# Feed-forward slots issued in pairs: two up products, then two down products, in one fixed order on TensorE

## The chip, the cores and the metric

The kernel runs on one core of one Trainium2 chip. The metric is the device time of one execution in microseconds (us), lower is better. Five engines work side by side, each through its own instructions in a fixed order: PE (TensorE, matrix products), ACT (ScalarE), DVE (VectorE), POOL (GpSimd) and SP (SyncE, which only issues transfers). They wait for one another by semaphores.

## The reference

Attention over 8 batches, 8 heads, 576 positions and 64 features, with a mask that is local (32 back) for the first four heads and strided (every 32nd position) for the others; its output becomes 4608 tokens of 512 features, which go through a feed-forward layer with a squared ReLU.

```python
scores = scale * np.matmul(q, k.transpose(0, 1, 3, 2))
mask_local = (rel >= 0) & (rel < stride)
mask_strided = (rel >= 0) & (pos[None, :] % stride == pos[:, None] % stride)
...
x = attn_out.transpose(0, 2, 1, 3).reshape(B * S, H * D)   # 4608 x 512
h = np.maximum(x @ w_in, 0.0)                              # w_in 512 x 2048
return h * h @ w_out                                       # w_out 2048 x 512
```

## The kernel before

The 4608 tokens are cut into 12 chunks of 384, and the 2048 hidden features into 16 tiles of 128. One chunk with one tile is a slot; slot s = 16 c + j belongs to chunk c and tile j, and there are 192 of them. float32 values are split into a high and a low part (x into xlh, xll, xsh, xsl: l for the local heads, s for the strided ones, the last letter for the part; weights and hidden values in the same way), and each product is made of three matmuls: high by high, high by low, low by high.

- `up(c, j)`, called U(s) in this text, makes the hidden tile h of a slot: 12 matmuls of 384 columns on PE (line 430) into one PSUM bank, then on ACT a relu (435), a square (436) and a copy to gh (437), then on DVE gl = h - gh (438). The bank is `j % 2` in chunk 0, so two banks in turn, and one of three in later chunks. gh and gl come from `gpool`, which holds two of each.
- `down(c, j)`, D(s), multiplies gh and gl with w_out: 9 matmuls of 512 columns (line 450) into three PSUM banks y that gather the 16 slots of the chunk. After the last slot of a chunk, DVE and ACT copy y out (454) and SP issues the three output transfers.
- The attention of chunk c+1 is made while chunk c goes through the feed-forward layer. The local heads (`pe_head`: matmuls s on line 231 and o on line 273, and around them ACT, DVE and POOL) and the strided ones (`strided`: products on POOL, pq and pp, sums on DVE) are generators; after each slot the loop advances them by a share.
- In chunk 0 the loop also converts the weights (`convert`): on ACT a first step z (162), a scaling of raw words (150) and a copy w (169), two steps on DVE (165, 166) and one on POOL (170), two cuts of 512 columns per slot.

What the program writes is then put in order by a list scheduler: on each engine it takes what is ready in its own estimate, and among that what was written first. So the loop's order gives priorities, not a fixed sequence. Down products lag by two slots:

```python
for s in range(NS + 2):
    c, j = divmod(s, NFT)
    if s < NS:
        up(c, j)
    if s >= 2:
        down(*divmod(s - 2, NFT))
    # then: weights in chunk 0, and a share of the attention of chunk c + 1
```

Of the kernel before, what the change touches and what calls it, by code (L numbers as in the profile page):

```python
# [23 lines left out]
TC = 384  # L24
WP = 512
NCHUNK = NT // TC
NFT = DF // P
# [20 lines left out]
def f32(ap):  # L48
    return ap.bitcast(F32)
# [23 lines left out]
def ranges(c):  # L73

    res = []
    for s, (b, g) in enumerate(SEGS[c]):
        if res and res[-1][0] == b and res[-1][2] == SI * g:
            res[-1][2] += SI
        else:
            res.append([b, SI * g, SI * (g + 1), SEG * s])  # L80
    return res
# [3 lines left out]
def attn_moe(ctx: ExitStack, tc, qk_l, v_l, qk_d, v_d, qk_p, v_p, f_s, q_s, k_s, v_s, w_in, w_out, masks, eye, out):  # L85
    nc = tc.nc
# [13 lines left out]
    def psum(i, nm):  # L100

        return ps.tile([P, 512], F32, name=nm, tag=f"ps{i}")
# [16 lines left out]
    last = {}  # L119
# [298 lines left out]
    g_tiles, y_ps = {}, {}  # L418

    def up(c, j):  # L420
        x = xt[c]
        p, o = divmod(j, 2)
        ph = psum(j % 2 if c == 0 else (c * NFT + j) % 3, f"h{c}_{j}")
        n = 0
        for kt in range(4):
            kind, kk = "ls"[kt // 2], kt % 2
            xh, xl = x[kind, "h"][:, kk, :], x[kind, "l"][:, kk, :]
            wsl = slice(kt * 256 + o * P, kt * 256 + (o + 1) * P)
            for w, xx in ((wi[p][0], xh), (wi[p][0], xl), (wi[p][1], xh)):
                nc.tensor.matmul(ph[:, :TC], w[:, wsl], xx, start=n == 0, stop=n == 11)  # L430
                n += 1
        gh = gpool.tile([P, TC], F32R, name=f"gh{c}_{j}", tag="gh")
        gl = gpool.tile([P, TC], F32R, name=f"gl{c}_{j}", tag="gl")
        g = ph[:, :TC]
        nc.scalar.activation(g, g, AF.Relu)  # L435
        nc.scalar.activation(g, g, AF.Square)  # L436
        nc.scalar.copy(gh, g)  # L437
        nc.vector.tensor_sub(gl, g, f32(gh))  # L438
        g_tiles[c, j] = gh, gl

    def down(c, j):
        gh, gl = g_tiles.pop((c, j))
        p, o = divmod(j, 2)
        if j == 0:
            y_ps[c] = [ps_y.tile([P, DM], F32, name=f"y{c}_{t}", tag="psy") for t in range(NTT)]
        wsl = slice(o * DM, (o + 1) * DM)
        for t in range(NTT):
            sl = slice(t * P, (t + 1) * P)
            for k, (g, w) in enumerate(((gh, wo[p][0]), (gh, wo[p][1]), (gl, wo[p][0]))):
                nc.tensor.matmul(y_ps[c][t], g[:, sl], w[:, wsl], start=j == 0 and k == 0, stop=j == NFT - 1 and k == 2)  # L450
        if j == NFT - 1:
            for t in range(NTT):
                y = ypool.tile([P, DM], F32, name=f"ysb{c}_{t}", tag="ysb")
                (nc.scalar.copy if t == 1 else nc.vector.tensor_copy)(y, y_ps[c][t])
                nc.sync.dma_start(out=out[c * TC + t * P : c * TC + (t + 1) * P, :], in_=y)


    def run(gen):
        for _ in gen:
            pass  # L460

    def behind(ins, gen):

        while True:
            with ExitStack() as st:
                for i in ins.values():
                    st.enter_context(tc.issue_after(i.ins))
                try:
                    k = next(gen)
                except StopIteration:  # L470
                    return
            yield k
# [25 lines left out]
    def local(c):  # L498
        if c < NPLAIN:
            heads = [pair_at(c, pr, True, pr, "34") for pr in range(2)]  # L500
            turns = (0, 0, 1, 0, 1, 0, 0, 1, 1, 1)
        else:
            heads = [pe_head(c, h) for h in range(HL)]

            turns = [0] * 3
            for h in range(HL):
                turns += [h] + [h + 1] * (3 if h + 1 < HL else 0) + [h] * 2
        for h in turns:
            next(heads[h])
            yield  # L510
# [53 lines left out]
    NS = NCHUNK * NFT  # L564
    for s in range(NS + 2):
        c, j = divmod(s, NFT)
        if s < NS:
            up(c, j)
        if s >= 2:
            down(*divmod(s - 2, NFT))  # L570
        if c == 0:
            for _ in range(WRATE):
                if next(weights, "end") != "end":
                    weights_end = {e: last[e] for e in "agsv"}
        if c + 1 < NCHUNK:
            if j == 0:
                lo, st = local(c + 1), strided(c + 1)
                if c == 0:
                    lo, st = behind(heads_end, lo), behind(heads_end, st)
                if c == 1:  # L580
                    lo, st = behind(weights_end, lo), behind(weights_end, st)
                cost = sum(2 * sum(range(i0 + 1, i1 + 1)) + 10 for _, i0, i1, _ in ranges(c + 1))
                dl = ds = 0
            fl, fs = ((j + 1) / n for n in SPREAD[min(c, 1)])
            while dl < fl * (10 if c + 1 < NPLAIN else 6 * HL) and next(lo, "end") != "end":
                dl += 1
            while ds < fs * cost:
                k = next(st, "end")
                if k == "end":
                    break  # L590
                ds += k
            if j == NFT - 1:
                run(lo)
                run(st)
# [76 lines left out]
```

## Time and profile before

| | |
|---|---|
| median of 3 runs | 903.3 us (903.24 to 903.33) |
| the profiled execution, its own time | 902.66 us |
| its span | 900.8 us |
| PE busy | 886.3 us (98%) |
| POOL busy | 693.4 us (77%) |
| DVE busy | 669.5 us (74%) |
| ACT busy | 564.4 us (63%) |
| granted PE clock, mean | 0.982 of full speed |

The span runs from the first to the last instruction; the profiled execution took 1.9 us more than its span. In rows of single groups a time stands before the engine; "x2" means two instructions of that kind in a row, and what stands in square brackets is the idle time before them and what ended it.

### The profile page before, as it was taken

The page shows a single profiled execution, that of the slowest core. Times are in us where ns is not written, and L with a number is a line of the kernel's source. Part 1 is how long each engine was busy: PE and PEld are TensorE (multiplying, and loading weights), DVE is VectorE, ACT ScalarE, POOL GpSimd, SP SyncE. Part 2 cuts the span into 40 slices and gives each one's busy share as a digit, 9 for nine tenths or more (in the row PEclk, how much of TensorE's full clock was granted, in tenths as well). Part 3 has the DMA queues.
Part 4 walks back from the last instruction along what each step waited for, and adds up shares of the span by engine and source line. Part 5 has one row for each costly group of instructions (what it writes and reads, how often), then busy time and mean ns, then how long its engine had stood idle before and what let it go on. Part 6 is the DMA issues. An engine that isn't in the chain of part 4 may idle for free.

```text
span 900.8 us, 14866 instructions
## 1 busy us (share of the span) xinstructions
PE 886.3 (98%) x4744; PEld 800.0 (89%) x4744; DVE 669.5 (74%) x1840; ACT 564.4 (63%) x1458; POOL 693.4 (77%) x724
## 2 busy tenths in 40 slices
PE   8989999999999999999999999999999999999997
PEld 7778899999999999999989989999999999999996
DVE  6789668878877878878878887887886887885111
ACT  3898967657657657747746755755665765764332
POOL 5788577788788889989879997988899799785000
PEclk8599999999999999999999999999999999999999
DMA  9833441323113114102212311221131111000000
GB/s 352 346 123 126 129 150 35 121 69 104 51 51 112 47 48 139 43 13 98 75 32 69 104 31 54 59 86 60 28 110 47 46 46 68 25 1 2 35 1 35
DMA packets 26798, 71.41 MB, mean 79 GB/s; under 512 B 2976, under 2 KB 8736, under 8 KB 25184
## 3 DMA queue, kind: packets, MB, share of 16 engines
q1 hardware_dynamic: 26432, 70.14, 23.4%
q8 instruction: 37, 0.61, 0.3%
q10 hardware_dynamic: 288, 0.33, 0.1%
q14 instruction: 41, 0.34, 0.1%
HBM read 61.01 MB, written 9.44 MB: 78 GB/s over the span
## 4 chain that ended last, share of the span: by engine, by line
PE 86%; POOL 5%; DVE 5%; ACT 2%; issue 1%; DVEq 0%; POOLq 0%; ACTq 0%
PE h L430 41%; PE y L450 40%; POOL pp L402 2%; PE s L231 2%; PE o L273 2%; POOL pq L380 1%; DVE sc L381 1%; DVE px L263 1%; PE b L308 1%; DVE p_t L256 1%; PE w_ps L525 1%; PE b L335 0%; POOL kx L215 0%; DVE e L312 0%; DVE nm L313 0%
## 5 line engine op out<-in xcount | busy, mean ns | idle before, releaser
L450 PE MATMUL y<-w,gh 128*128 128x512 f32 x1152 | 361.9, 395 | 2.4 <-ACT gh L437 2.4
L450 PEld LDWEIGHTS y<-w,gh 128*128 128x128 f32 x1152 | 212.6, 189 | 35.0 <-ACT gh L437 2.6
L430 PE MATMUL h<-xlh,w 128*128 128x384 f32 x768 | 232.7, 342 | 0.4 <-DVE xsl L351 0.4
L430 PE MATMUL h<-xsh,w 128*128 128x384 f32 x768 | 228.1, 337 | 0.0
L402 POOL TENSOR_TENSOR pp<-vs,sc 128x448 f32<-128x448 f32 (+10 forms) x192 | 193.6, 1034 | 39.9 <-issue 21.7
L450 PE MATMUL y<-w,gl 128*128 128x512 f32 x576 | 223.7, 395 | 0.0
L380 POOL TENSOR_TENSOR pq<-ks,qs 128x512 f32<-128x512 f32 (+2 forms) x192 | 200.1, 1063 | 16.0 <-DVE sc L381 12.4
L381 DVE TENSOR_REDUCE sc<-pq 128x8 f32<-128x512 f32 (+4 forms) x228 | 120.1, 535 | 61.4 <-POOL pq L380 59.7
L435 ACT ACTIVATE h<-h 128x384 f32<-128x384 f32 x192 | 91.0, 475 | 112.6 <-PE h L430 111.5
L438 DVE TENSOR_TENSOR gl<-h,gh 128x384 fp32r<-128x384 f32 x192 | 105.4, 549 | 61.4 <-ACT gh L437 59.9
L430 PEld LDWEIGHTS h<-xlh,w 128*128 128x128 f32 x768 | 142.9, 189 | 8.4 <-DVE xsl L351 0.7
L430 PEld LDWEIGHTS h<-xsh,w 128*128 128x128 f32 x768 | 142.5, 189 | 0.5 <-ACT w L169 0.3
L403 DVE TENSOR_REDUCE qs<-pp 128x64 f32<-128x448 f32 (+11 forms) x192 | 106.8, 563 | 31.7 <-POOL pp L402 29.6
L430 PE MATMUL h<-xll,w 128*128 128x384 f32 x384 | 130.3, 339 | 0.0
L430 PE MATMUL h<-xsl,w 128*128 128x384 f32 x384 | 129.2, 336 | 0.0
L450 PEld LDWEIGHTS y<-w,gl 128*128 128x128 f32 x576 | 108.0, 188 | 20.8
L437 ACT CAST gh<-h 128x384 fp32r<-128x384 f32 x192 | 91.2, 475 | 34.1 <-PE y L450 30.3
L436 ACT ACTIVATE h<-h 128x384 f32<-128x384 f32 x192 | 91.0, 474 | 4.5
L240 ACT ACTIVATE e<-e,nm 96x128 f32<-96x128 f32 x160 | 62.6, 392 | 28.3 <-DVE nm L223 27.0
L430 PEld LDWEIGHTS h<-xll,w 128*128 128x128 f32 x384 | 72.8, 190 | 7.5
L256 DVE STREAM_TRANSPOSE p_t<-e 32x128 f32<-32x128 f32 x240 | 72.2, 301 | 4.8 <-ACT e L245 1.4
L430 PEld LDWEIGHTS h<-xsl,w 128*128 128x128 f32 x384 | 72.7, 189 | 0.2
(82 smaller groups left out, 1113.6 us busy)
## 6 DMA issues: line engine op xcount, KB each, us to landing
qk<-qk_l SPq DMA_DIRECT2D x24, 400.0 KB, 3.1
y<-ysb SPq DMA_DIRECT2D x36, 256.0 KB, 2.3
raw<-w_in SPq DMA_DIRECT2D x7, 1024.0 KB, 11.1
qk<-qk_l SPq DMA_DIRECT2D x16, 416.0 KB, 3.1
vs<-v_s SPq DMA_DIRECT2D x10, 576.0 KB, 3.8
raw<-w_out SPq DMA_DIRECT2D x5, 1024.0 KB, 13.3
v<-v_l SPq DMA_DIRECT2D x40, 128.0 KB, 2.0
ks<-k_s SPq DMA_DIRECT2D x8, 576.0 KB, 3.7
```

Of the source, the lines that this page charges most:

```text
L240: nc.scalar.activation(e[:QC, cut(w)], e[:QC, cut(w)], AF.Exp, bias=nmax[:QC, w : w + 1], scale=-1.0, accum_out=ssum[:QC, w, :1])
L256: nc.vector.transpose(out=pt[STR * k : STR * (k + 1), :, STR * r : STR * (r + 1)], in_=e.rearrange("p (w k) -> p w k", k=KW)[STR * r : STR ...
L380: nc.gpsimd.tensor_mul(pv, kt[:, a : a + m, :], qt[:, i - i0 : i - i0 + 1, :].broadcast_to([P, m, D]))
L381: nc.vector.tensor_reduce(out=sc[:, i - i0, a : a + m], in_=pv, op=ALU.add, axis=AX.X)
L402: nc.gpsimd.tensor_mul(pv, vt[:, a : a + nd, :n], sc[:, il : il + 1, :n].broadcast_to([P, nd, n]))
L403: nc.vector.tensor_reduce(out=ot[:, il, a : a + nd], in_=pv, op=ALU.add, axis=AX.X)
L430: nc.tensor.matmul(ph[:, :TC], w[:, wsl], xx, start=n == 0, stop=n == 11)
L435: nc.scalar.activation(g, g, AF.Relu)
L436: nc.scalar.activation(g, g, AF.Square)
L437: nc.scalar.copy(gh, g)
L438: nc.vector.tensor_sub(gl, g, f32(gh))
L450: nc.tensor.matmul(y_ps[c][t], g[:, sl], w[:, wsl], start=j == 0 and k == 0, stop=j == NFT - 1 and k == 2)
```

## The change

The loop now issues at every even s two up products, U(s) and U(s+1), and then two down products, D(s-2) and D(s-1). Each group of two is written inside `tc.issue_after` of the last matmul of the group before it, which makes the scheduler put all of the group's instructions on PE behind that one. For that, `up` and `down` return their last matmul. Inside a group the scheduler is still free, and so it is with the attention's instructions. The weights and the attention are advanced after each s as before.

```diff
-        if s < NS:
-            up(c, j)
-        if s >= 2:
-            down(*divmod(s - 2, NFT))
+
+        if s % 2 == 0:
+            for part, slots in (up, (s, s + 1)), (down, (s - 2, s - 1)):
+                with ExitStack() as behind_last:
+                    if "ff" in last:
+                        behind_last.enter_context(tc.issue_after(last["ff"].ins))
+                    for i in slots:
+                        if 0 <= i < NS:
+                            last["next"] = part(*divmod(i, NFT))
+                last["ff"] = last["next"]
```

In the rows below a name is a tile with chunk and slot (h0_2 is the hidden tile of chunk 0, slot 2; gh0_0, gl0_0 the split one of slot 0), followed by a running number. Line 450 of before is line 451 now.

On PE, at the first slots, behind U(0), U(1) and four matmuls of attention (b), before:

```order
L308 MATMUL b11_0_1_619<-qk1_0_1_552 96x128 x4
L450 MATMUL y0_0_663<-w1_0_421,gh0_0_532 128x512 x2
L450 MATMUL y0_1_664<-w1_0_421,gh0_0_532 128x512 x2
L450 MATMUL y0_2_665<-w1_0_421,gh0_0_532 128x512 x2
L430 MATMUL h0_2_644<-xlh0_435,w0_1_407 128x384
L430 MATMUL h0_2_644<-xll0_436,w0_1_407 128x384
```

and at the same place now:

```order
L308 MATMUL b11_0_1_619<-qk1_0_1_571 96x128 x4
L430 MATMUL h0_2_644<-xlh0_435,w0_1_407 128x384
L430 MATMUL h0_2_644<-xll0_436,w0_1_407 128x384
L430 MATMUL h0_2_644<-xlh0_435,w0_1_407 128x384 x2
L430 MATMUL h0_2_644<-xll0_436,w0_1_407 128x384
L430 MATMUL h0_2_644<-xlh0_435,w0_1_407 128x384
```

The six matmuls of D(0) with gh have moved from ahead of U(2) to behind U(3); U(2) writes the bank that U(0) used.

On ACT, in chunk 0 from the relu of slot 5 on, before:

```order
L435 ACTIVATE h0_5_830<-h0_5_830 128x384
L162 ACTIVATE z8_512_868<-raw8_680 128x512
L169 CAST w1_3_858<-raw8_680 128x512
L436 ACTIVATE h0_5_830<-h0_5_830 128x384
L437 CAST gh0_5_843<-h0_5_830 128x384
```

and now:

```order
L435 ACTIVATE h0_5_779<-h0_5_779 128x384
L162 ACTIVATE z8_512_868<-raw8_708 128x512
L169 CAST w1_3_858<-raw8_708 128x512
L436 ACTIVATE h0_5_779<-h0_5_779 128x384
L437 CAST gh0_4_773<-h0_4_760 128x384
```

The copy gh of slot 4, which stood ahead of the relu of slot 5, now stands behind relu, z, w and square of slot 5; gh of slot 5 comes four instructions later.

On PE, at the border from chunk 3 to chunk 4 (h4_0 is U(64), y3 with gh3_14 is D(62)), before:

```order
L430 MATMUL h4_0_3920<-xlh4_3248,w0_0_395 128x384
L430 MATMUL h4_0_3920<-xll4_3249,w0_0_395 128x384
L430 MATMUL h4_0_3920<-xlh4_3248,w0_0_395 128x384 x2
L450 MATMUL y3_0_3222<-w1_7_1270,gh3_14_3877 128x512 x2
L450 MATMUL y3_0_3222<-w1_7_1270,gl3_14_3878 128x512
L450 MATMUL y3_1_3223<-w1_7_1270,gh3_14_3877 128x512 x2
L430 MATMUL h4_0_3920<-xll4_3249,w0_0_395 128x384
```

and now:

```order
L430 MATMUL h4_0_3920<-xlh4_3276,w0_0_395 128x384
L231 MATMUL s05_0_4020<-kx5_0_3991,qx5_0_3990 96x256 x2
L231 MATMUL s25_0_4026<-kx5_0_3991,qx5_0_3990 96x256 x2
L430 MATMUL h4_0_3920<-xlh4_3276,w0_0_395 128x384
L430 MATMUL h4_1_3939<-xlh4_3276,w0_0_395 128x384
L430 MATMUL h4_1_3939<-xll4_3277,w0_0_395 128x384
L430 MATMUL h4_1_3939<-xlh4_3276,w0_0_395 128x384 x2
L430 MATMUL h4_0_3920<-xll4_3277,w0_0_395 128x384
```

The five matmuls of D(62) that stood inside U(64) are gone from there; four of U(65) and the s matmuls of the next chunk's first head stand in their place.

More of the change, by code (lines that the diff above doesn't have):

```diff
@@ L429, in up @@
             for w, xx in ((wi[p][0], xh), (wi[p][0], xl), (wi[p][1], xh)):
-                nc.tensor.matmul(ph[:, :TC], w[:, wsl], xx, start=n == 0, stop=n == 11)
+                done = nc.tensor.matmul(ph[:, :TC], w[:, wsl], xx, start=n == 0, stop=n == 11)
                 n += 1
@@ L439, in up @@
         g_tiles[c, j] = gh, gl
+        return done
     def down(c, j):
@@ L449, in down @@
             for k, (g, w) in enumerate(((gh, wo[p][0]), (gh, wo[p][1]), (gl, wo[p][0]))):
-                nc.tensor.matmul(y_ps[c][t], g[:, sl], w[:, wsl], start=j == 0 and k == 0, stop=j == NFT - 1 and k == 2)
+                done = nc.tensor.matmul(y_ps[c][t], g[:, sl], w[:, wsl], start=j == 0 and k == 0, stop=j == NFT - 1 and k == 2)
         if j == NFT - 1:
@@ L455, in down @@
                 nc.sync.dma_start(out=out[c * TC + t * P : c * TC + (t + 1) * P, :], in_=y)
+        return done
     def run(gen):
```

## The prediction

> **What bounds the kernel now.** U(s) and D(s) are the twelve up matmuls and the nine down matmuls of slot s. I read the page first.
>
> ```profile
> span 900.8 us, 14866 instructions
> ...
> PE 886.3 (98%) x4744; PEld 800.0 (89%) x4744; DVE 669.5 (74%) x1840; ACT 564.4 (63%) x1458; POOL 693.4 (77%) x724
> ...
> PE 86%; POOL 5%; DVE 5%; ACT 2%; issue 1%; DVEq 0%; POOLq 0%; ACTq 0%
> ```
>
> PE is busy for 98% of the span, and 86% of the chain of waits is PE. A busy PE can hide pauses, so the windows (after its span each row has busy us and count by engine, then PE's granted clock) and PE's waits came next.
>
> ```profile
> 46.00:61.00 15.00, 12.64 (x64) 11.07 (x64) 13.39 (x31) 12.98 (x25) 11.15 (x13) 0.89 0.31 99
> 61.00:71.00 10.00, 10.00 (x54) 8.36 (x53) 8.62 (x19) 10.00 (x20) 10.00 (x13) 1.00 0.65 222
> 116.00:186.00 70.00, 70.00 (x368) 63.66 (x367) 54.91 (x174) 45.71 (x128) 55.82 (x67) 1.00 0.29 92
> 824.00:901.00 77.00, 71.69 (x357) 64.24 (x355) 11.96 (x21) 24.48 (x52) 1.32 (x1) 0.98 0.06 21
> ```
>
> ```profile
> PE y L450 <- ACT gh L437: 2.4, 1, 2.4
> ...
> PE o L273 <- DVE px L263: 1.3, 1, 1.3
> ```
>
> From 61 us on PE never rests within these windows; behind its start it waits twice worth naming, 2.4 us for gh(0) and 1.3 us for an attention head. Whatever makes PE wait anywhere is therefore paid in full, and at most 3.7 us can be won back. Last, the spacing of matmuls where no attention is left:
>
> ```profile
> 851.52 0.33 PE L430 MATMUL h<-xsh,w 128*128 128x384 f32 x1
> 851.69 0.63 PE L450 MATMUL y<-w,gh 128*128 128x512 f32 x2
> ...
> 853.54 0.39 PE L450 MATMUL y<-w,gl 128*128 128x512 f32 x1
> 853.77 0.33 PE L430 MATMUL h<-xlh,w 128*128 128x384 f32 x1
> ```
>
> U to D takes 0.17 us from start to start and D to U 0.23, which is (853.77-851.69)/9 = 0.23 again: a change from U to D costs nothing. U takes 12 x 0.175 = 2.1 us, D 2.08.
>
> **The change part by part.** No instruction is added or removed. Half the joins between U and D go (192 of them): worth 0 by the rows above. What changes is what stands between a producer and its consumer. gpool holds two gh and two gl, so gh(s) on ACT waits for the end of D(s-2) in either version. In chunk 0 two PSUM banks hold h, so U(s+2) waits for gl(s). Before, U(s+1) and D(s-1) lay in between, 4.2 us; now only D(s-1) does, 2.08 us.
>
> *A, the start.* U(2) now stands ahead of D(0), and needs the bank that gl(0) frees.
>
> ```profile
> 48.69 0.48 ACT L437 CAST gh<-h 128x384 fp32r<-128x384 f32 x1
> ...
> 49.23 2.93 PE L450 MATMUL y<-w,gh 128*128 128x512 f32 x6 [2.35 <-ACT gh L437]
> ...
> 50.88 0.55 DVE L438 TENSOR_TENSOR gl<-h,gh 128x384 fp32r<-128x384 f32 x1
> ...
> 51.96 0.42 PE L430 MATMUL h<-xlh,w 128*128 128x384 f32 x1
> ```
>
> ```profile
> 45.30:48.70 3.40, 1.57 (x11) 1.11 (x10) 1.79 (x4) 3.27 (x9) 1.41 (x2) 1.00 0.22 54
> 48.70:52.10 3.40, 2.87 (x7) 2.30 (x8) 3.40 (x9) 2.57 (x6) 2.31 (x2) 0.50 0.19 73
> 52.10:55.50 3.40, 3.40 (x20) 3.18 (x19) 3.33 (x11) 2.85 (x6) 2.63 (x3) 1.00 0.31 46
> ```
>
> ACT and DVE have the same order up to gl(0), which ends at 50.88+0.55 = 51.43. So U(2) starts near 51.5. At 51.96 the six matmuls of D(0) are missing (6 x 0.23 = 1.4 us at full clock) and 0.46 us of U(2) at half clock (0.2) are there: 1.2 us lost. Then the clock: a stretch of 3.4 us with PE busy for 1.57 was followed by one at 0.50, one with 2.87 by one at 1.00. Now 48.7 to 52.1 holds some 0.6 us, so 52.1 to 55.5 should run at half clock: 3.4/2 = 1.7 us more. Bounds: 1.2 (the clock comes up anyway) and 4.6 (one more such stretch). I take 1.2+1.7 = 2.9, since 0.6 is nearer to 1.57 than to 2.87. The Trainium skill's page "TensorE: Matmul & The Clock Gate", section "What's actually happening", has the clock fall only after an idle window of about 3.4 us. Here it fell behind a window that was 46% busy, so the row decides; by the page A would be 1.2 and the whole sum 1.7 us less.
>
> *B, the other bank waits of chunk 0*, U(4) to U(15), twelve of them. How late gl(s) comes behind the end of D(s-2), at the shortest (s=9) and the longest (s=8) of slots 2 to 15:
>
> ```profile
> 88.57 0.86 PE L450 MATMUL y<-w,gl 128*128 128x512 f32 x3
> 89.78 0.48 ACT L437 CAST gh<-h 128x384 fp32r<-128x384 f32 x1
> 90.30 0.56 DVE L438 TENSOR_TENSOR gl<-h,gh 128x384 fp32r<-128x384 f32 x1
> ...
> 83.16 0.86 PE L450 MATMUL y<-w,gl 128*128 128x512 f32 x3
> 86.60 0.47 ACT L437 CAST gh<-h 128x384 fp32r<-128x384 f32 x1
> 89.10 0.52 DVE L438 TENSOR_TENSOR gl<-h,gh 128x384 fp32r<-128x384 f32 x1
> ```
>
> ```profile
> L169 ACT CAST w<-raw 128x512 fp32r<-128x512 f32 x24 | 15.7, 652 | 0.0
> L162 ACT ACTIVATE z<-raw 128x512 uint32<-128x512 uint32 x23 | 14.6, 636 | 2.4 <-DVE raw L166 2.4
> L435 ACT ACTIVATE h<-h 128x384 f32<-128x384 f32 x16 | 7.8, 486 | 6.0 <-PE h L430 6.0
> ```
>
> That is 90.86-89.43 = 1.4 us and 89.62-84.02 = 5.6 us. Against 2.08 us of cover the shortest costs 0, the longest 3.5: bounds 0 and 12 x 3.5 = 42. Much of the long one goes, because relu and square of slot s now run under U(s+1) and D(s-2) and only gh and gl are left: gh 0.48, gl 0.55, half an instruction in flight on each engine (0.33, 0.28), hand-overs 0.15, together 1.8, just under the cover. But ACT is full here (10.00 of 10.00 us). In the pairs 2, 4, 8 and 12 a relu of slot s+1, a z and a w stand between square(s) and gh(s): from the end of U(s+1), 0.48+0.65+0.64 = 1.8 and in three of them a square of 0.48, so ACT reaches gh(s) about when D(s-2) ends, if it began on time, and any lateness of ACT is PE's. I let one release in each of four pairs wait for one more ACT instruction, 0.7 us: 2.8. It is nearer to the short end.
>
> *C, chunk borders.* Before, D(s-2) could run between the matmuls of U(s) when x of the new chunk was late; now U(s+1) stands ahead of it. POOL's last write of x against PE, chunks 7 to 8 and 3 to 4:
>
> ```profile
> 612.33 1.02 POOL L281 TENSOR_TENSOR xll<-e,xlh 64x384 fp32r<-64x384 f32 x1
> ...
> 613.26 0.63 PE L450 MATMUL y<-w,gh 128*128 128x512 f32 x2
> ...
> 614.88 0.34 PE L430 MATMUL h<-xll,w 128*128 128x384 f32 x1
> ```
>
> ```profile
> 326.52 1.01 POOL L281 TENSOR_TENSOR xll<-e,xlh 64x384 fp32r<-64x384 f32 x1
> ...
> 328.62 0.63 PE L450 MATMUL y<-w,gh 128*128 128x512 f32 x2
> ```
>
> Without the filler PE would need xll at 613.26, 0.1 us before it is there, and at 328.62, 1.1 us after. By the order, the last head's o stands 1.9 and 3.4 us of U and D work later than before there; the new chunk's s matmuls (0.5) and in the second case four of U(s+1) (0.7) fill. That leaves 0.1+1.9-0.5 = 1.5 and 3.4-1.1-0.5-0.7 = 1.1. The tightest of the other borders is the last, where the strided part of x is late:
>
> ```profile
> 823.48 1.85 POOL L414 TENSOR_TENSOR xsl<-ks,xsh 128x768 fp32r<-128x768 f32 x1 [1.88 <-ACT xsh L413]
> ...
> 825.49 0.63 PE L450 MATMUL y<-w,gh 128*128 128x512 f32 x2
> ```
>
> It lands at 825.33, 0.16 us before PE would need it without filler; six of U(177) now fill 1.05, and PE's lag of A and B gives POOL, which has a queue of its own here, more room. Minus the 1.3 us of PE's wait for o, which stands twelve matmuls later: C = 1.3, from -1.3 to 8 (eleven borders of 0.7).
>
> *No price:* in later chunks three banks hold h and the tighter release has 4.2 us of cover; on SP's queue the output transfers keep their places, and loads of q and k pass them by one to three places, mostly forward; nothing of U or D runs on POOL. ACT now often waits for two D in a row with gh(s) and gh(s+1), and attention's exps queue behind; ACT is busy 45.71 of 70.00 there, so I count its price in C alone.
>
> Sum: 2.9+2.8+1.3 = 7.0 us. The profiled execution took 902.66 us, 0.64 under the median of the runs, 903.30: 902.66+0.64+7.0 = 910.3.
>
> **The rivals.**
> - *No change.* The clock is up at 52.1, no release in B is late and C is 0: 903.3+1.2 = 904.5. For it: the 1.8 us under the cover. Against: ACT at 10.00 of 10.00. It is in force when gl(s) comes within 2.08 us each time.
> - *Faster.* A join costs up to 0.01 us, the last digit of the rows: 192 x 0.01 = 1.9, and the wait for o goes, 1.3: 903.3-3.2 = 900.1. It decides once A and B together are under 1.4 us, which needs gl(0) right behind gh(0), near 49.8. DVE has other work there.
> - *ACT's lag carries over.* Every release of B waits as the middle slot of before would (3.8 us late, less 2.08, 1.7): 12 x 1.7 = 20 instead of 2.8, 927. For it: ACT was full. Against: relu and square are out of that chain.
> - *The clock falls in chunk 0.* If waits bunch until a 3.4 us stretch is as empty as the one with 1.57, each costs 1.7 us; three of them, 5.1: 915. Against: my waits leave over 2.6 of 3.4 busy, near the 2.87 that kept the clock. The Trainium skill's same page, section "A second HAM failure mode: psum-queue depth-cycling", tells of short pauses between groups of matmuls that cycle through PSUM banks and make the clock swing; no run shown here has it.
>
> **How the numbers follow.** Forecast 0.63 (its own range 906 to 915), no change 0.13, faster 0.06, lag 0.09, clock 0.09. From 903.5 to 918 lie the forecast, no change and the clock, 0.8 in all with some loss at the edges. Under 0.2% (1.8 us) this kernel's times can't tell a change from none: faster 0.06, same 0.13, slower 0.81.
>
> **What would show it.** A: PE waits for DVE gl(0) until about 51.5, and the clock is 0.50 to about 55. B: PE h waits for DVE gl, a few us over chunk 0, ACT full. C: PE h waits for POOL xll at 613 and 328 plus the lag. Wrong would be: U(2) starting before 50; PE without waits from 56 to 120; spacings other than 0.175 and 0.23; or ACT's blocking making attention late at every border.

## The result, and the profile after

The changed kernel takes 908.4 us (median of 4 runs, 906.94 to 909.46) against 903.3 us (903.24 to 903.53) for the kernel before: a ratio of 1.0055, 95% interval 1.0038 to 1.0072, 5.1 us slower. The forecast was 910.3. Its profiled execution took 908.41 us, with a span 5.8 us longer than before; the rows below are of that execution.

The head of the page, and the chain of waits by engine:

```profile
span 906.6 us, 14784 instructions
...
PE 884.3 (98%) x4744; PEld 799.5 (88%) x4744; DVE 666.8 (74%) x1840; ACT 558.6 (62%) x1458; POOL 690.3 (76%) x724
...
PE 69%; DVE 11%; POOL 9%; ACT 5%; issue 4%; DMA 2%; SPq 0%; DVEq 0%; POOLq 0%; ACTq 0%
```

PE is busy for 2.0 us less than before in a span that is 5.8 us longer. So PE works a little less and rests 7.8 us more, and the chain now runs through DVE, POOL and ACT for a quarter of its length. The windows around the start of chunk 0 (same columns as before):

```profile
45.30:48.70 3.40, 0.78 (x8) 0.56 (x6) 2.94 (x6) 3.37 (x8) 2.68 (x3) 1.00 0.45 122
48.70:52.10 3.40, 1.41 (x4) 1.42 (x5) 3.40 (x9) 3.40 (x8) 2.05 (x3) 0.65 0.02 6
52.10:55.50 3.40, 3.40 (x12) 3.40 (x12) 3.30 (x10) 2.37 (x6) 2.90 (x4) 0.50 0.50 130
55.50:59.00 3.50, 3.50 (x17) 3.26 (x16) 2.78 (x7) 3.50 (x7) 3.50 (x6) 0.85 0.42 176
```

The clock is at half speed over all of 52.1 to 55.5, where it was full before. What PE waits for there, from the order of time:

```profile
50.08 0.55 DVE L438 TENSOR_TENSOR gl<-h,gh 128x384 fp32r<-128x384 f32 x1
...
50.69 0.69 PE L430 MATMUL h<-xlh,w 128*128 128x384 f32 x1 [4.61 <-DVE gl L438]
```

U(2) waits 4.6 us for gl(0) and starts right behind it. Two lists of PE's waits follow, for the whole span and then from 120 us on:

```profile
PE h L430 <- DVE gl L438: 8.6, 8, 4.6
...
PE h L430 <- DVE gl L438: 2.7, 4, 0.9
PE h L430 <- POOL xll L281: 1.8, 1, 1.8
PE o L273 <- DVE px L263: 0.7, 1, 0.7
```

So of the 8.6 us for gl, 4.6 lie at U(2), 1.3 in the rest of chunk 0, and 2.7 in later chunks, where three banks hold h. Last, the spacing where no attention is left. First before, the starts of U(182) and U(184), then after, the same two slots:

```profile
849.59 0.33 PE L430 MATMUL h<-xlh,w 128*128 128x384 f32 x1
...
857.96 0.33 PE L430 MATMUL h<-xlh,w 128*128 128x384 f32 x1
```

```profile
856.14 0.33 PE L430 MATMUL h<-xlh,w 128*128 128x384 f32 x1
...
864.45 0.33 PE L430 MATMUL h<-xlh,w 128*128 128x384 f32 x1
```

By the starts themselves, with one digit more than the rows have, two slots took 8.374 us before and take 8.306 now. No wait lies in either stretch. Half as many joins between U and D make each pair of slots 0.07 us shorter.

From these traces, the account of the difference by stage. The first matmuls of U(16) and U(176) are counted off in PE's order (the 193rd and the 2113th matmul of line 430), and at U(16) the same D, up to D(13), are done in both. First before, then after:

```profile
116.08 0.33 PE L430 MATMUL h<-xlh,w 128*128 128x384 f32 x1
...
824.43 0.33 PE L430 MATMUL h<-xlh,w 128*128 128x384 f32 x1
```

```profile
120.91 0.33 PE L430 MATMUL h<-xlh,w 128*128 128x384 f32 x1
...
831.22 0.33 PE L430 MATMUL h<-xlh,w 128*128 128x384 f32 x1
```


| stage | before | after | difference |
|---|---|---|---|
| up to the start of U(16) | 116.1 | 120.9 | +4.8 |
| U(16) to U(176), chunks 1 to 10 | 708.3 | 710.3 | +2.0 |
| from U(176) to the start of D(191)'s last matmul | 70.9 | 70.3 | -0.6 |
| behind it | 5.5 | 5.1 | -0.4 |
| span | 900.8 | 906.6 | +5.8 |

In chunks 1 to 10 the shorter joins give 4.3 us (the spacings of U and D that hold no wait, summed over all of them), and 6.2 us of waits take it back. The long gaps between U's matmuls and the next ones (over 0.25 us, counted above the usual 0.175) grew from 1.8 to 4.2 us in sum. The time from each attention matmul to the next matmul grew from 35.5 to 39.2 us in sum, since most of these waits stand right behind attention's matmuls.

### The profile page after: what moved, and what is told of

It reads as the page before. It is cut to its first block, busy times and chain, and to the rows that moved or that the text cites. A ratio compares the mean times of both kernels' runs of the same rounds, so it can differ in the third digit from the quotient of the medians.

```text
span 906.6 us, 14784 instructions
## 1 busy us (share of the span) xinstructions
PE 884.3 (98%) x4744; PEld 799.5 (88%) x4744; DVE 666.8 (74%) x1840; ACT 558.6 (62%) x1458; POOL 690.3 (76%) x724
## 4 chain that ended last, share of the span: by engine, by line
PE 69%; DVE 11%; POOL 9%; ACT 5%; issue 4%; DMA 2%; SPq 0%; DVEq 0%; POOLq 0%; ACTq 0%
PE h L430 33%; PE y L451 32%; POOL pq L380 4%; DVE p_t L256 2%; POOL pp L402 2%; DVE gl L438 1%; DVE sc L381 1%; PE s L231 1%; DVE qs L403 1%; PE o L273 1%; DMA raw<-w_in 1%; POOL xll L281 1%; ACT e L240 1%; ACT e L245 1%; POOL qx L217 1%
## 5 line engine op out<-in xcount | busy, mean ns | idle before, releaser
L451 PE MATMUL y<-w,gh 128*128 128x512 f32 x1152 | 357.0, 391 | 0.0
```

The source lines that it names most:

```text
L451: done = nc.tensor.matmul(y_ps[c][t], g[:, sl], w[:, wsl], start=j == 0 and k == 0, stop=j == NFT - 1 and k == 2)
```

## The experiments

**Is it the order of writing, or the tie?** One kernel keeps the pairs but not the tie to the group before; another ties single slots.

```diff
-                    if "ff" in last:
+                    if False:
```

> The pairs are written as in the change, but nothing ties one group behind the other, so the scheduler may again reorder U and D on PE. Main theory (the loss is waits that the fixed order forbids PE to fill: 2.8 us at the start, some 2 in the rest of chunk 0, 2 at the border to chunk 4, 3 at three-bank releases): the built order of chunk 0 is that of before, D(0) ahead of U(2), and D fills the releases later, so nearly all is back, 903.3 to 904.5 us. Rival 1 (the pairs as such cost, since a bank release has one D less of cover whatever the order): 906 to 908. Rival 2 (any new schedule of this size is worth a few us by chance): anywhere from 902 to 909.

It took 908.82 us, ratio 1.0060 (1.0046 to 1.0074): the main theory and the first rival were missed, and only the rival that any new schedule is worth a few us by chance covers it. Without the tie PE's order in chunk 0 is that of before, and PE is only 0.6 us behind at the end of that chunk. The loss comes later, from about 450 us on. PE's longest waits from 122 us on:

```profile
PE o L273 <- DVE px L263: 3.4, 4, 2.1
PE h L430 <- DVE gl L438: 1.2, 2, 0.7
PE h L430 <- POOL xsl L414: 1.1, 1, 1.1
```

Most of it is waiting for attention (px and xsl, 4.5 us). Merely writing the slots in twos, which changes priorities and nothing else, makes attention late.

```diff
-        if s % 2 == 0:
-            for part, slots in (up, (s, s + 1)), (down, (s - 2, s - 1)):
+        groups = [(up, (s,)), (down, (s - 2,))]
+        for part, slots in groups:
```

> The other half: one up, one down as before, each tied behind the one before it. Main theory: U(2) stands ahead of D(0) again, so the start costs its 2.8 us; the bank releases of chunk 0 have two parts of cover again (4.2 us) and cost 0 to 1; at chunk borders D cannot fill U, 1 to 2 us: 906 to 908. Rival 1 (pairs cost, the fixed order does not): 903.3 to 904. Rival 2 (chance): anywhere from 902 to 909.

It took 910.1 us, 1.0071 (1.0058 to 1.0083), above all three expected ranges. Tied singles are no cure. The start is better: U(0) is done ahead of U(1), so U(2) starts at 46.58 us, and at 60 to 90 us PE is some 4 us ahead of the kernel before. By 121 us that is gone: PE waits 2.1 us for POOL's and ACT's share of the weights and 1.1 for gl, and the rest lies in shorter gaps. Later strided attention is late:

```profile
PE h L430 <- POOL xsl L414: 4.3, 2, 2.9
```

**Which part of the program pays?** The first kernel has the old loop in chunk 0 and fixed pairs from slot 16 on; the second has fixed pairs up to slot 17 and the old loop behind.

```diff
-        if s % 2 == 0:
+        if s < NFT:
+            last["next"] = up(c, j)
+            if s >= 2:
+                last["next"] = down(*divmod(s - 2, NFT))
+        elif s % 2 == 0:
```

> Chunk 0 in the old way (one up, one down, free), fixed pairs from chunk 1 on. Main theory: the lag of 4.5 us that PE has at the end of chunk 0 goes, what later chunks lose (2 us of x at borders, some 3 at three-bank releases, less what dips give back) stays: 904 to 906. Rival 1 (the pairs cost in each chunk alike): 907.5 to 908.5, since eleven of twelve chunks keep them. Rival 2 (chance): 902 to 909.

It took 905.48 us, 1.0019 (1.0010 to 1.0028): within the main theory's range, but not for its reason, as the rows below show.

```diff
-        if s % 2 == 0:
+        if s > NFT + 1:
+            if s < NS:
+                last["next"] = up(c, j)
+            last["next"] = down(*divmod(s - 2, NFT))
+        elif s % 2 == 0:
```

> The complement: fixed pairs in chunk 0 (and the two slots behind it), one up and one down, free, afterwards. Main theory: the 4.5 us of chunk 0 stay and nothing is added: 907 to 908.5; with the run before it in this batch the two losses add up to that of the whole change within 1 us. Rival 1 (cost spread over all chunks): 903.5 to 904.5. Rival 2 (chance): 902 to 909 and no adding up.

It took 908.91 us, 1.0056 (1.0044 to 1.0069). The pairs of chunk 0 alone bring a loss as large as that of the whole change: U(16) starts 5.2 us late and the lag stays. That is 0.4 us above the expected range. The expectation also had the two losses add up to that of the whole change, 5.1 us, within 1 us; they are 1.8 and 5.2, together 7.0. The pairs of the later chunks do better than the total of 905.48 says. With the old chunk 0, U(16) to U(176) took 703.9 us, 4.4 less than before, and U(176) began 3.6 us earlier than before. Then PE ran into attention. PE at U(176) and U(177) in that kernel, and the windows there:

```profile
826.91 0.61 PE L430 MATMUL h<-xsh,w 128*128 128x384 f32 x2 [3.85 <-ACT xsh L413]
828.80 0.69 PE L430 MATMUL h<-xsl,w 128*128 128x384 f32 x1 [1.28 <-POOL xsl L414]
```

```profile
821.60:825.00 3.40, 1.46 (x9) 1.14 (x7) 2.74 (x7) 0.00 (x0) 3.01 (x4) 1.00 0.00 0
825.00:828.40 3.40, 0.61 (x2) 0.30 (x2) 0.96 (x2) 0.83 (x1) 1.46 (x1) 1.00 0.00 0
828.40:831.80 3.40, 3.00 (x9) 3.00 (x10) 0.00 (x0) 0.95 (x2) 0.35 (x1) 0.50 0.00 0
```

The waits and the half clock behind them cost 7.0 us together, more than the pairs had won.

**What would the pairs give if attention were in time?** Three kernels leave out the last four rows of the strided scores of chunk 11, so that its strided x is ready sooner: the changed kernel, the one with the old chunk 0, and the kernel before as a control.

```diff
-            for i in range(i0, i1):
+            for i in range(i0, i1 - (4 if c == NCHUNK - 1 else 0)):
```

> The whole change, but the last four rows of the strided scores of chunk 11 are left out (some 9 us of POOL's work; the order up to chunk 10 is the same), so that the last strided x comes early. Two-limit theory (PE's own waits lag it by some 6 us by chunk 11; attention's last x, at 833.4 us, comes just as PE gets there and adds nothing): stays at 907.5 to 908.5 us. Rival (what costs is attention, made late by ACT and DVE blocking on gh and gl; PE's waits only fill time that it would lose anyway): falls to 903 to 905.5.

> Chunk 0 in the old way, fixed pairs afterwards, with the same four rows of scores of chunk 11 left out. Without the cut PE was 3.6 us ahead of before at chunk 11 and then waited 3.9 and 2.0 us for the strided x, with a stretch at half clock. Two-limit theory: the waits go, 899 to 901 us: fixed pairs cost PE nothing behind chunk 0, and attention's last x (828.7) is the limit of that kernel. Rival (pairs cost PE in later chunks): 904 to 905.5.

> The kernel before, with the same four rows of scores of chunk 11 left out: a control for the cut. PE did not wait at chunk 11 (the last x landed 0.16 us before PE could have needed it), so both theories say no change, 902.8 to 903.6 us. If it falls by more than 1 us, attention held the kernel before in a way that its waits do not show.

The changed kernel with this cut took 908.82 us (1.0055, 1.0041 to 1.0069); what follows for it rests on this time alone. The one with the old chunk 0 took 898.69 us (0.9944, 0.9931 to 0.9956). The control took 903.5 us (0.9999, 0.9990 to 1.0008). The first two lie 0.3 us above and 0.3 us below the ranges of the two-limit theory, far from the rivals', and the control is in its range. So the last strided x costs neither the kernel before nor the changed one anything, and the 5 us of the changed kernel have come about before PE reaches it. Attention in earlier chunks is not touched by this cut. With the old chunk 0 and nothing to wait for at U(176), fixed pairs give 5.0 us. These are all of PE's waits from 122 us on that are left there:

```profile
PE h L430 <- POOL xsl L414: 0.8, 1, 0.8
PE h L430 <- DVE gl L438: 0.7, 2, 0.5
```

**Can the start be mended?** U(0) is tied ahead of U(1), which frees its bank sooner.

```diff
-            for part, slots in (up, (s, s + 1)), (down, (s - 2, s - 1)):
+            for part, slots in ((up, (0,)), (up, (1,))) if s == 0 else ((up, (s, s + 1)), (down, (s - 2, s - 1))):
```

> The whole change, but at the very start U(0) is tied ahead of U(1), so that gl(0) is ready sooner: in the run with fixed singles U(2) then started at 46.6 us without waiting and PE was 4.5 us ahead of before. PE's own path should be 2.8+4.5 = 7.3 us shorter at slot 4. Two-limit theory: attention does not get earlier by as much, its last x near 833 holds PE, 905 to 908. Rival (only PE's path counts): 901 to 902.

It took 913.35 us, 1.0105 (1.0092 to 1.0119): both expected ranges were missed on the slow side. The start came near what was expected: when U(5) and D(3) are done PE is 5.8 us earlier than in the changed kernel (7.3 expected), U(16) starts 1.2 us late instead of 4.8, and at 754 us PE is 0.9 us ahead of the kernel before. Then it stops for chunk 10's local heads. PE's two longest waits from 122 us on and the windows there:

```profile
PE o L273 <- DVE rs L241: 6.5, 1, 6.5
PE s L231 <- POOL qx L217: 3.3, 1, 3.3
```

```profile
755.00:759.30 4.30, 1.04 (x8) 0.72 (x6) 3.23 (x16) 2.46 (x12) 4.14 (x5) 1.00 0.00 0
759.30:773.00 13.70, 6.54 (x23) 5.67 (x22) 12.26 (x40) 8.78 (x27) 13.09 (x14) 0.50 0.27 83
```

POOL (13.09 of 13.70) and DVE (12.26) are full while PE waits, and 13.7 us at half clock come on top.

**Is POOL the limit behind PE?** Head 3's scaling moves from POOL (10 instructions of 1.04 us) to ACT, in the kernel with the old chunk 0, in the kernel before as control, and in the one with U(0) first. A fourth kernel also moves the subtraction for the low half of v from POOL to DVE.

```diff
-        if h != HL - 1:
+        if h < HL:
```

```diff
-        nc.gpsimd.tensor_sub(vx[:, :, 1, :], vr, f32(vx[:, :, 0, :]))
+        nc.vector.tensor_sub(vx[:, :, 1, :], vr, f32(vx[:, :, 0, :]))
```

> Chunk 0 in the old order, fixed pairs from chunk 1, and the scaling of head 3's weights (10 instructions of 1.04 us on POOL) moved to ACT as for the other heads (4 of 0.32 each). Theory 'POOL's attention chain is the second limit': xsl of chunk 11 ended at 828.7 us where PE was ready at about 823; with 1 us less POOL work in each of ten chunks it ends 3 to 10 us earlier, U(176) and U(177) no longer wait 5.9 us, and the time comes to 899 to 901.5. Rival 'what is late is ACT's or DVE's work and not POOL's': 905 to 906.5, since ACT gets 12.8 us more work.

> The kernel of the run before, and the subtraction that makes the low half of v (40 of 0.76 us on POOL) moved to DVE. If POOL alone is the second limit, xsl of chunk 11 ends still earlier and the time is 898.5 to 900.5, PE's own path by the run with the cut scores (898.7). If DVE shares the limit (it is busy for 52 to 58 of each 70 us), gl comes later, PE h waits for DVE gl, and it is 1 to 4 us slower than the run before.

> Control: the kernel before with head 3's scaling moved from POOL to ACT. Before, xsl of chunk 11 ended 0.16 us ahead of PE's need and PE hardly waited, so POOL's relief has nothing to give: 902.7 to 904, the same for both theories. A gain of 2 us or more here would say that the relief itself, not the order of pairs, is what makes the run of this call with the old chunk 0 faster.

> The changed kernel with U(0) tied ahead of U(1), and head 3's scaling on ACT. With POOL's work as it is this kernel took 913.35: to 754 us it was 0.9 us ahead of the kernel before, then PE waited 3.6 and 6.9 us for chunk 10's heads (POOL qx, then o) and ran 13.7 us at half clock. Theory 'POOL is the second limit': with 10 us less on POOL those waits go at least in part, and the time is 901 to 907. Rival 'the wait at 755 us comes from the order of the pairs itself': 911 to 915.

| kernel | median, us | ratio to before | 95% interval |
|---|---|---|---|
| old chunk 0, scaling on ACT | 904.24 | 1.0009 | 1.0000 to 1.0018 |
| the same, and v on DVE | 924.82 | 1.0240 | 1.0225 to 1.0256 |
| before, scaling on ACT | 902.11 | 0.9984 | 0.9975 to 0.9993 |
| U(0) first, scaling on ACT | 915.90 | 1.0134 | 1.0120 to 1.0148 |

My theory that POOL alone is the second limit fails in three of these four, and the rivals' ranges were missed there too: the second kernel lost some 20 us against the first where its rival had 1 to 4. The control came out 0.6 us below its expected range. It has no wait of PE from 122 us on, so the 1.3 us for o, which the kernel before waits once, are gone, which is about what it gained. In the control POOL's relief did what it should to attention: xsl of chunk 11 (line 414 on POOL) started at 823.48 before, and with the relief

```profile
812.87 2.20 POOL L414 TENSOR_TENSOR xsl<-ks,xsh 128x768 fp32r<-128x768 f32 x1 [1.54 <-ACT xsh L413]
```

10.6 us earlier, for 10.4 us less work on POOL. But the same relief in the kernel with the old chunk 0 brought

```profile
825.35 1.84 POOL L414 TENSOR_TENSOR xsl<-ks,xsh 128x768 fp32r<-128x768 f32 x1 [0.82 <-ACT xsh L413]
```

which is 1.6 us earlier than the 826.94 of that kernel without it. The border at U(176) is free there now, as expected, but PE waits elsewhere. All of PE's waits from 122 us on, of the kernel with the old chunk 0 and the relief, and the four longest of the one that also moves v:

```profile
PE h L430 <- DVE gl L438: 4.1, 6, 1.4
PE o L273 <- DVE px L263: 0.2, 1, 0.2
```

```profile
PE h L430 <- DVE gl L438: 8.4, 11, 1.5
PE s L231 <- POOL qx L217: 3.5, 1, 3.5
PE h L430 <- POOL xsl L414: 2.9, 1, 2.9
PE s L231 <- DVE e L278: 2.2, 2, 1.2
```

In these two kernels, though not in the control, work taken from POOL and given to ACT or DVE comes back as waits for gl, which is made on ACT and then DVE (without the relief PE waited 0.3 us for gl there). So POOL alone is not the second limit. That ACT's and DVE's queues, in which attention and feed-forward stand behind one another, have a part in it is read from these waits and not shown by a run of its own. The waits of ACT for PE at gh (line 437), between 122 and 825 us, show one way. In this order: before, after, old chunk 0, pairs in chunk 0 alone, before with the relief, old chunk 0 with the relief.

```profile
ACT gh L437 <- PE y L450: 16.4, 26, 1.2
```

```profile
ACT gh L437 <- PE y L451: 55.3, 56, 1.6
```

```profile
ACT gh L437 <- PE y L451: 50.0, 54, 1.6
```

```profile
ACT gh L437 <- PE y L451: 18.3, 29, 0.9
```

```profile
ACT gh L437 <- PE y L450: 9.3, 16, 0.9
```

```profile
ACT gh L437 <- PE y L451: 34.3, 39, 1.6
```

Where fixed pairs run in the later chunks, ACT stands 25 to 39 us longer in its queue for the end of D(s-2), with attention's exps behind it. xsl of chunk 11 is then ready later: it ends at 833.4 in the changed kernel and at 826.2 with pairs in chunk 0 alone, although PE is equally late in the two (U(176) starts at 831.2 and 831.0). That these waits are the cause is likely but not shown: with tied singles ACT waits only 21.1 us there, and xsl also ends at 833.4. A third gh and gl in `gpool`, which would take these waits away, was not run.

**The fastest kernel that does all the work** has none of the pairs: the kernel before with head 3's scaling on ACT, 902.11 us. Its gain is 1.4 us, and the interval's lower end is 0.07%. That is less than the 0.2% under which the prediction called a change and none alike, so it is small and barely to be told from nothing.

## Why the prediction was right, and where it was not

The forecast of 7.0 us more than before came out 1.9 us too high, within its range, with the sign it gave 0.81. Term by term, with the lag of PE at equal numbers of U and D matmuls:

- **A, the start: predicted 2.9, measured 2.8** (PE's lag when U(3) and D(1) are done, at 57.4 us). Both halves came as worked out, and each a little different. U(2) started at 50.69 and not at 51.5, because DVE reached gl(0) 0.8 us earlier than before (50.08 against 50.88); that is 1.5 us behind the 49.23 at which PE went on before. The clock had fallen by 49.7 already, inside PE's wait, and came up only at 56.5, so PE worked 5.9 us at half clock instead of 2.9, which costs 1.5 us more. PE rested from 46.1 to 50.7 without a break. So here the rule of the Trainium skill's page "TensorE: Matmul & The Clock Gate", section "What's actually happening", that the clock falls behind one idle window, gives the half clock as well as my row does; that the sum by it would be 1.7 us less was wrong, since I had not seen the wait that long. The size of this term is in part chance. The control with the relief has PE's order of before at the start, and there the half clock lasted from 48.1 to 54.9, where the profile before shows 48.7 to 52.1; U(16) started at 117.4 instead of 116.1. The Trainium skill's page "TensorE: Matmul & The Clock Gate", section "What's actually happening", says that the windows of the monitor run freely and do not start with the kernel; these two traces agree. Eight of the profiled executions have this same order on PE up to U(16), and U(16) starts between 116.1 and 117.5 in them; the profile of before is the earliest. The two with pairs in chunk 0 start it at 120.9 and 121.3, so at least 3.4 us of the lag in these profiles belong to the order.
- **B, the banks in chunk 0: predicted 2.8, measured 2.0** (4.8 at U(16), less 2.8). Only three releases waited for gl in a way that the list of waits shows, U(10), U(14) and U(15) with 1.3 us in all, of the four that I had wait for 0.7 each. Of the rest 0.4 is a wait for POOL's e, and 0.3 is in no list of waits. The mechanism and the sign were right, and the size was within 0.8 us.
- **C, the borders: predicted 1.3.** U(64) waited 1.8 us for xll instead of 1.1. U(128) waited 0.1 instead of 1.5: four s matmuls of the next head and four of its own filled the place, and xll was in time. The wait for o, which I had taken out with 1.3, stays at 0.7. In sum that is 1.3 again (1.8+0.1-0.6), from other parts than mine, which is luck.
- **"No price" in later chunks: this step failed.** Three-bank releases were said to have 4.2 us of cover, but four of them waited 2.7 us in all. At U(35), behind a border:

```profile
200.03 0.47 ACT L437 CAST gh<-h 128x384 fp32r<-128x384 f32 x1
...
201.21 0.64 DVE L455 COPY ysb<-y 128x512 f32<-128x512 f32 x1
...
201.88 1.25 DVE L256 STREAM_TRANSPOSE p_t<-e 32x128 f32<-32x128 f32 x4
...
203.16 0.56 DVE L438 TENSOR_TENSOR gl<-h,gh 128x384 fp32r<-128x384 f32 x1
...
203.77 0.44 PE L430 MATMUL h<-xlh,w 128*128 128x384 f32 x1 [0.74 <-DVE gl L438]
```

  D(30) ended at 198.4, ACT took up gh(32) 1.6 us later, and it was ready at 200.50. DVE was then summing scores, copied y and transposed p, and took up gl 2.7 us later, so that gl(32) came 5.3 us behind the end of D(30). My cover was measured against gh and gl alone and left out what ACT and DVE have in their queues at a border. A and B were near because there I had looked at the queues.
- **"A join costs nothing": this step failed, and in the kernel's favour.** I had read the interval at the seam itself, 0.17 and 0.23 us, and it is indeed the usual one. The cost is spread over the matmuls behind the seam: in the last chunk, by the starts of PE's matmuls, the first U behind a D takes 2.106 us and one behind a U 2.080; the first D behind a U 2.081 and one behind a D 2.040. That is 26 and 41 ns, 0.067 us for each pair of slots. Chunks 1 to 10 won 4.3 us by it and chunk 11 0.6. The rival "faster" had put at most 1.9 us on the joins, with an end at 0.01 us each; they are worth 0.034 each where nothing else runs on PE. With it falls "at most 3.7 us can be won back": with the old chunk 0 and the cut, fixed pairs gave 5.0.

So the sum was near by luck, because two missed terms stood against each other: 4.9 us won by joins in chunks 1 to 11, and in chunks 1 to 10 6.2 us of waits where I had 1.3. The rows for A and B, 5.7 predicted and 4.8 measured, carry the verdict, and the pairs in chunk 0 alone give the same loss. The waits in chunks 1 to 10 do not belong to pairs as such. With the old chunk 0 the same pairs have the long gaps of U at 1.2 us and the spacing of attention at 36.1, near the 1.8 and 35.5 of before. Only chunk 0 is written otherwise there, and yet 179 of the 320 matmuls s and o stand at another place among U and D: what the list scheduler does in chunk 0 changes how attention is woven in for the rest of the program. So the rival of the first experiments, that any new schedule is worth a few us by chance, is not ruled out for the later chunks. Which of the scheduler's choices makes a border late was not settled. Nor was why U(0) first leaves chunk 10's heads so late; POOL's scaling is not the reason, since with it moved that kernel took 915.9.

The rival "ACT's lag carries over" did not come (927), nor did the clock fall a second time in chunk 0. "Wrong would be spacings other than 0.175 and 0.23" was the sentence that should have led to a sum over many slots.

## What to carry to other kernels

Price a reordering by the length of a whole period where nothing waits (here 8.374 against 8.306 us for two slots), not by the one interval at the seam. Before a tie moves a consumer nearer to its producer, list what the producer's engine has in its queue at that place, in each stage: the start and the borders paid here, the steady stretch did not. A kernel whose bound engine is 98% busy may have another chain a few tenths of a microsecond behind it (0.16 us at the last border here), so that a true gain on the first engine can come to nothing until that chain is moved too. And judge a change of order by stages: a schedule that is new in one place is new behind it as well.

## What the hardware showed that was not expected

- In the last chunk, a change between the two kinds of matmul groups (384 columns into one PSUM bank, 512 columns into another) cost 26 ns from the second kind to the first and 41 ns from the first to the second. It is spread over the next six to nine matmuls and not paid at the change.
- Waits of 3 to 4 us in a late chunk were followed by half speed: with the old chunk 0 by 3.4 us of it at U(177), a loss of half that. With U(0) first the clock stayed at half for 13.7 us, with PE busy for 6.54 of them; within that time PE rested for 6.5 us in one go (the wait for rs in the list above).
- The 3.4 us ahead of the half clock need not be idle. In the kernel before, PE's wait for gh(0) ran from 46.9 to 49.2 us, so PE had rested for only 1.8 us when the clock fell at 48.7. With tied singles it fell at 760.5 behind a single wait of 2.9 us. The Trainium skill's page "TensorE: Matmul & The Clock Gate", section "What's actually happening", has the fall only behind an idle window of about 3.4 us; these two disagree. At U(176) with the old chunk 0 the stretch ahead of the fall held 0.61 us of work in 3.40, but PE had rested for 3.85 us in one go, from 823.1 to 826.9, so that row alone would not decide. How much work keeps the clock up was not settled, and its share of the last 3.4 us alone does not say it: 1.46 us kept it up at 821.6 to 825.0 of that run, 1.57 us did not at 45.3 to 48.7 of the kernel before, and 1.91 us did not in the kernel that also moves v:

```profile
693.28:696.69 3.41, 1.91 (x8) 1.08 (x7) 2.56 (x5) 2.64 (x6) 3.33 (x3) 1.00 0.22 85
696.69:700.10 3.41, 3.02 (x9) 3.02 (x10) 2.29 (x13) 1.71 (x9) 3.33 (x5) 0.50 0.55 173
```
